# A fused recurrence and router kernel: embeddings scaled on ScalarE, tables built in the first turns, K's copy moved ahead, one idle product less

## The chip, the cores and the metric

The kernel runs on one core of one Trainium2 chip. The metric is the device time in microseconds (us), the median of several runs. Engines are named as in the profile: PE is TensorE (matmuls; PEld its weight loads), DVE is VectorE, ACT is ScalarE, POOL is GpSimd, SP is SyncE, which here issues most DMAs.

## The reference

Two blocks follow each other. The first is a linear recurrence with decay, for 4 batches, 8 heads, 768 steps and a head size of 48:

```
for t in range(S):
    cur = u * k[t] (outer) v[t]
    y[t] = r[t] @ (state + cur)
    state = w * state + k[t] (outer) v[t]
```

Its output, as 3072 tokens of 384 numbers, goes to a cosine router with 8 experts:

```
xn = x / (norm(x) + 1e-6);  en = emb / (norm(emb) + 1e-6)
logits = xn @ en.T / tau;   expert = argmax(logits)
gate = softmax(logits)[expert]
out = gate * (relu(x @ w1[expert]) @ w2[expert])
```

All is in fp32. What matters for the change is `en / tau`: the 8 rows of embeddings, each divided by its norm and by tau.

## The kernel before

The sequence is cut into 6 chunks of 128 steps; chunk and batch make 24 units. `attention` (line 842) walks over them in turns i = -1 to 23, and in each turn it writes out, by hand, the order in which the engines get their work for several units at once. Each engine works through its own instructions strictly in that order. `build_first` (line 49) comes ahead of turn -1 and starts the loads, the powers of the decay and unit 0's first products.

In turn i the pieces that matter here are, in the order of the code:

- `turn_r(i+1)`: PE turns R (L355) into a PSUM bank, DVE multiplies it by the powers (RT, L357).
- `own_rows(i, 0)` and `own_rows(i, 1)`: ACT multiplies V by the diagonal terms, four heads each (L341, four instructions). The result xd is read by `rows`.
- `turn_k(i+1)`: PE turns K (L364) into the bank "st", ACT copies it to KT (L373). That bank is also the one that `states` writes, so `states` waits for the copy.
- `scaled(i+2)` and `own(i+2)`: three POOL products of 128x384 (L312, L323, L327).
- `squares`: ACT squares rows of X (L558) for the norms, in turns 4 to 6 two a turn.
- `own_sum(i+1)`: DVE sums KU (L332).
- `sums(i)`: PE forms y (L438 with the carried state from turn 4 on, L447 with AT), ACT copies it to yT (L452).
- `states(i)`: PE (L404), into the bank "st".
- `carry(i)`: DVE adds the state (L417 or L419), POOL decays it (L420).
- `scores(i+1)`: PE (L383), 16 products. `masked(i+1, 0 and 1)`: DVE, AT (L389), twice.
- `rows(i)`: PE turns yT back (L465), DVE adds xd and writes X (L471).
- `turn_rows(i-1)`: PE turns X (L551), ACT copies it to xT (L553).

Every four turns a group of 4 units is routed: logits (L567), `choose` and `before` (DVE, L590 to L612), ranks, places, norms and lists, spread over the turns that follow. From turn 19 on the experts' weights are loaded, and after the last turn `experts` (line 1366) works through the 8 experts, almost only on PE.

Two small preparations are Python generators. Each `next` emits one step at that point of the order.

- `emb = build_experts(k)` (L233): squares and norm of the embeddings, the scaling, three PE transposes (L249) and a copy to `ent` (L250), which logits read. The steps go out in turns 1, 3 and 4.
- `tables = build_turned(k)` (L191): `no_counts` (L215, L216), `bits` (L197 to L199), `own` (L201, L202), `mask` (L205), `turned` (L206, L207) and `tie` (L210). They are all on DVE and serve the ordering of the experts in turns 19 to 21. `cum` is first read in turn 6. The steps go out in turns 4 and 5.

WAKE (line 40) is the number of idle products (L67) of 512 columns that PE does in the lead-in while the first loads are under way; each becomes two instructions.

Of the kernel before, what the change touches and what calls it, by code (L numbers as in the profile page):

```python
# [13 lines left out]
ALU = mybir.AluOpType  # L14
# [3 lines left out]
B, H, S, D = 4, 8, 768, 48  # L18
# [18 lines left out]
W_MIN, W_MAX = 0.7, 1.4  # L37
TS = 32
TG = TT // TM
WAKE = 3  # L40
AHEAD = 5
SQUARES = {1: (), 2: (), 3: (), 4: (0, 1), 5: (2, 4), 6: (3, 5)}

# [5 lines left out]
def build_first(k):  # L49
# [15 lines left out]
    def busy(columns):  # L65
        ps = k.ps.tile([128, 512], F32, name="wake", tag="y")
        nc.tensor.matmul(ps[:, 0:columns], k.ones, wide[:, 0:columns], start=True, stop=True)  # L67

    for _ in range(WAKE):
        busy(512)  # L70
# [120 lines left out]
def build_turned(k):  # L191


    nc, pool = k.nc, k.const
    no_counts(k)
    bits = pool.tile([2 * QS, 3], I32, name="bits")
    nc.vector.tensor_scalar(bits[:, 0:1], k.part, 2, E - 1, ALU.arith_shift_right, ALU.bitwise_and)  # L197
    nc.vector.tensor_scalar(bits[:, 1:2], k.part, 3, None, ALU.bitwise_and)
    nc.vector.tensor_scalar(bits[:, 2:3], k.part, 3, 4, ALU.arith_shift_right, ALU.bitwise_and)  # L199
    own = pool.tile([2 * QS, 3], F32, name="own")  # L200
    nc.vector.tensor_copy(own, bits)  # L201
    nc.vector.tensor_add(own[:, 1:2], own[:, 1:2], own[:, 2:3])  # L202
    yield
    k.mask = pool.tile([2 * QS, E], F32, name="mask")
    nc.vector.tensor_scalar(k.mask, k.number, own[:, 0:1], None, ALU.is_equal)  # L205
    nc.vector.scalar_tensor_tensor(k.turned, k.qt, own[:, 1:2], k.turned, ALU.is_equal, ALU.mult)  # L206
    nc.vector.tensor_scalar_add(k.turned, k.turned, -1.0)  # L207

    k.tie = pool.tile([128, E], F32, name="tie")
    nc.vector.tensor_scalar(k.tie, k.number, N + 1.0 / 16, None, ALU.mult)  # L210
    yield


def no_counts(k):
    k.nc.vector.memset(k.cum, 0.0)  # L215
    k.nc.vector.tensor_copy(k.cum[0:1, :], k.ebase)  # L216
# [16 lines left out]
def build_experts(k):  # L233

    nc, pool = k.nc, k.aconst
    emb, tau = k.emb_rows, k.tau_rows
    sq = k.work.tile([E, DM], F32, name="emb_sq", tag="sq")
    nrm = pool.tile([E, 1], F32, name="emb_nrm")
    nc.scalar.activation(sq, emb, ACT.Square, accum_out=nrm)
    nc.gpsimd.tensor_tensor(out=nrm, in0=nrm, in1=k.half[0:E, 0:1], op=ALU.pow)  # L240
    yield
    nc.vector.tensor_scalar_add(nrm, nrm, 1e-6)
    nc.vector.reciprocal(nrm, nrm)
    nc.vector.reciprocal(tau, tau)
    nc.vector.tensor_scalar(emb, emb, nrm, tau, ALU.mult, ALU.mult)
    yield
    ps = k.ps.tile([128, NK, E], F32, name="ps", tag="xp")
    for c in range(NK):
        nc.tensor.transpose(ps[:, c, :], emb[:, c * 128 : (c + 1) * 128], k.ident[0:E, 0:E])  # L249
    nc.vector.tensor_copy(k.ent[:, :, 0:E], ps)  # L250
    yield
# [78 lines left out]
def own_sum(k, i):  # L330
    diag = k.work.tile([128, H], F32, name="diag", tag="diag")
    k.nc.vector.reduce_sum(diag, k.KU.pop(i), axis=AX.X)  # L332
    k.diag[i] = diag


def own_rows(k, i, half):
    if half == 0:
        k.xd[i] = k.work.tile([128, H, D], F32, name="xd", tag="xd")
    diag, V = k.diag[i], k.loaded[i][2]
    for h in range(half * H // 2, (half + 1) * H // 2):  # L340
        k.nc.scalar.mul(k.xd[i][:, h, :], V[:, h, :], diag[:, h : h + 1])  # L341
# [290 lines left out]
def norms(k, g):  # L632
    k.nc.gpsimd.tensor_tensor(out=g.ssq, in0=g.ssq, in1=k.half, op=ALU.pow)
# [208 lines left out]
def attention(k):  # L842


    units = B * NCH

    def on(f, i, *more):
        if 0 <= i < units:
            f(k, i, *more)
# [5 lines left out]
    def whole(f, i, *more):  # L855
        if 0 <= i < units and i % B == B - 1:
            f(k, k.groups[i // B], *more)

    emb, tables = build_experts(k), build_turned(k)
    for i in range(-1, units):  # L860
        j = i - SETTLED * B
        if 0 < i + AHEAD < units:
            load(k, i + AHEAD)
        whole(places, i - 4)
        whole(logits_out, i - 3)
        if i >= 0:
            on(turn_r, i + 1)
        if i == 0:
            own_sum(k, i)
        if 0 < i < units - 1:  # L870
            on(own_rows, i, 0)
        if i >= 0:
            on(turn_k, i + 1)
        whole(turn_logits, i - 3)
        if i == B + 3:
            norms(k, k.groups[0])
        on(scaled, i + 2)
        if i < 0:
            own_r(k, 0)
        on(own, i + 2)  # L880
        for n in SQUARES.get(i, (i - 1,)):
            of_group(squares, n)
        if 0 < i < units - 1:
            on(own_rows, i, 1)
        if i > B + 1:
            whole(norms, i - 2)
        if j == 10:
            k.lists = turned_lists(k, perm, "tp")
            lists = taken_by_rank(k, k.lists)
            first = [Early(k, r, *lists, w) for r, w in zip(LAST, k.weights)]  # L890
        whole(choose, i - 3)
        whole(before, i - 3)
        whole(located, i - 4)
        whole(gates, i - 5)
        whole(lanes, i - 5)
        whole(listed, i - 5)
        if 0 <= i < units - 2:
            on(own_sum, i + 1)
        if i == B:
            next(emb)  # L900
        if j == 7:
            load_, count = loads(k, "xp")
        if j == 9:
            expert_of(k, by)
            number = expert_number(k, LAST[0])
            load_w1(k, number, k.weights[0][0])
        on(sums, i)
        on(states, i)
        for n in (0, 1) if i == 0 else ():
            own_rows(k, i, n)  # L910
        whole(taken, i - 6, "xp")
        whole(exps, i - 4)
        on(carry, i)
        whole(summed, i - 6)
        on(scores, i + 1)
        on(masked, i + 1, 0)
        if i == 0:
            masked(k, i + 1, 1)
        on(rows, i)
        if i != 0:  # L920
            on(masked, i + 1, 1)
        if i == units - 2:
            own_sum(k, i + 1)
            own_rows_once(k, i + 1)
        of_group(put, i)
        if j == 10:
            load_w2(k, number, k.weights[0][1])
        of_group(turn_rows, i - 1)
        whole(logits, i - 2)
        whole(ranks, i - 3)  # L930
        if i == 0:
            build_constants(k)
        if i in (1, 3):
            next(emb)
        if i in (B, B + 1):
            next(tables)
        if 3 <= i < 3 + len(k.ring):
            k.nc.gpsimd.memset(k.ring[i - 3], 0.0)
        if j == 8:
            by = order(k, load_)  # L940
        if j == 9:
            settle(k, by, count)
            perm = turner(k, by)
# [657 lines left out]
```

## Time and profile before

| | us |
|---|---|
| median of 3 runs (lowest, highest) | 408.53 (408.34, 410.69) |
| span of the profiled execution | 406.3 |
| PE busy | 388.5 |
| DVE busy | 256.2 |
| ACT busy | 172.0 |
| POOL busy | 160.5 |

A line of the timeline gives the start and the length in us, the engine, the line of the kernel, the operation, what it writes and reads with the shape, how many instructions are merged, and in brackets the idle time of the engine ahead of it and what ended it. For example the first idle products and the first scores:

```profile
1.64 4.97 PE L67 MATMUL wake<-wide,ones 128*128 128x512 f32 x6 [1.64 <-DVE wide L61]
...
8.42 1.16 PE L383 MATMUL at<-RT,KT 48*128 48x128 f32 x16 [0.18 <-DVE RT L357]
```

A line of the waits names the waiting engine, tile and line, then what ended the wait, then the total in us, how often, and the longest. Lengths of merged lines overlap at their ends, since instructions are pipelined; what a step costs its engine is the distance from its start to the next start.

### The profile page before, as it was taken

The numbers are of one execution on the slowest core, as the hardware profiler recorded it, in microseconds if no ns is written. First come the engines' busy times: TensorE is split into PE (matmuls) and PEld (weight loads), VectorE is DVE, ScalarE is ACT, GpSimd is POOL, SyncE is SP. The second block draws the span as 40 slices with busy tenths as digits, with TensorE's granted clock in tenths as the row PEclk, the third lists the DMA queues.
The fourth block names the chain that finished last, engine by engine and source line by source line (L and its number), as shares of the span: only waits on it lengthen the run. The fifth ranks groups of instructions, "written<-read, shape, count | busy, mean of one in ns | idle before, by whom it ended". The sixth has DMA issues, their size and how long they took to land.

```text
span 406.3 us, 9261 instructions
## 1 busy us (share of the span) xinstructions
PE 388.5 (96%) x3544; PEld 353.0 (87%) x3544; DVE 256.2 (63%) x604; ACT 172.0 (42%) x522; POOL 160.5 (40%) x215
## 2 busy tenths in 40 slices
PE   8979999999999999999999999999999999999980
PEld 5868888888888877899999999999999999799680
DVE  5777998878688770757667657367257266456310
ACT  3876876767677411432333232233233223232020
POOL 6996688767764332400602402401320330300220
PEclk9999999999999999999999999999999999999996
DMA  8999767767715982244706441614434340330101
GB/s 156 182 200 207 156 138 152 151 140 150 158 40 182 286 299 65 85 157 164 244 15 234 158 156 39 200 42 154 153 122 155 109 165 2 101 113 1 58 27 39
DMA packets 93800, 54.39 MB, mean 134 GB/s; under 512 B 76937, under 2 KB 88380, under 8 KB 93746
## 3 DMA queue, kind: packets, MB, share of 16 engines
q1 hardware_dynamic: 90242, 44.26, 41.0%
q0 software_dynamic: 3296, 9.44, 7.2%
q8 instruction: 30, 0.49, 0.5%
q14 instruction: 24, 0.20, 0.2%
q10 hardware_dynamic: 208, 0.00, 0.0%
HBM read 44.45 MB, written 9.63 MB: 133 GB/s over the span
## 4 chain that ended last, share of the span: by engine, by line
PE 85%; DVE 4%; SPq 3%; issue 3%; ACT 2%; DMA 1%; POOL 0%; POOLq 0%; ACTq 0%
PE ps L1217 25%; PE ps L1281 16%; PE ps L1321 5%; PE at L383 5%; PE y L447 4%; PE ps L1335 4%; PE early_h L1027 3%; PE early_y L1036 3%; PE ps L1195 3%; PE yrows L465 2%; PE y L438 2%; PE ps L1165 2%; PE rt L355 2%; PE st L404 2%; PE kt L364 2%
## 5 line engine op out<-in xcount | busy, mean ns | idle before, releaser
L1081 POOL DMA_INDIRECT out_dram<-y,to x25 | 30.0, 1199 | 173.7 <-issue 116.4
L1217 PE MATMUL ps<-xTe,w 128*128 128x192 f32 (+3 forms) x336 | 62.9, 327 | 0.0
L1217 PEld LDWEIGHTS ps<-xTe,w 128*128 128x128 f32 x336 | 55.9, 190 | 0.5
L341 ACT ACTIVATE xd<-V,diag 128x48 f32<-128x48 f32 x184 | 46.1, 324 | 0.0
L389 DVE TENSOR_TENSOR AT<-at,umask 128x512 f32<-128x512 f32 x48 | 32.7, 684 | 10.9 <-PE at L383 10.7
L1224 ACT ACTIVATE hT<-hT 128x384 f32<-128x384 f32 (+3 forms) x42 | 22.0, 523 | 32.4 <-DVE hT L1247 19.7
L1281 PE MATMUL ps<-Tw,Sh 128*128 128x192 f32 x192 | 32.5, 326 | 0.0
L1281 PEld LDWEIGHTS ps<-Tw,Sh 128*128 128x128 f32 x192 | 31.4, 190 | 0.0
L1072 POOL DMA_INDIRECT G<-xs,take x25 | 26.9, 1078 | 10.5 <-issue 4.0
L1217 PE MATMUL ps<-Tx,Sw 128*128 128x192 f32 (+3 forms) x168 | 29.7, 326 | 0.0
L383 PE MATMUL at<-RT,KT 48*128 48x128 f32 x384 | 27.9, 285 | 0.6 <-DVE RT L357 0.6
L1217 PEld LDWEIGHTS ps<-Tx,Sw 128*128 128x128 f32 x168 | 27.6, 190 | 0.1
L1234 DVE TENSOR_TENSOR u<-ps,p 128x384 f32<-128x384 f32 (+3 forms) x14 | 7.8, 558 | 31.3 <-ACT p L1231 16.6
L447 PE MATMUL y<-AT,V 128*48 128x128 f32 (+1 forms) x384 | 26.0, 278 | 0.0
L383 PEld LDWEIGHTS at<-RT,KT 48*128 48x128 f32 x384 | 23.3, 187 | 2.9 <-DVE RT L357 1.0
L327 POOL TENSOR_TENSOR KU<-KU,Rpad 128x384 f32<-128x384 f32 x24 | 24.1, 1003 | 1.8
L312 POOL TENSOR_TENSOR Kpad<-K,kpow 128x384 f32<-128x384 f32 x23 | 23.1, 1005 | 1.4 <-DVE kpow L110 1.4
L553 ACT COPY xT<-xp 128x384 f32<-128x384 f32 x24 | 11.5, 480 | 28.6 <-PE xp L551 28.6
L447 PEld LDWEIGHTS y<-AT,V 128*48 128x48 f32 (+1 forms) x384 | 19.9, 124 | 4.2 <-issue 3.6
L1281 PE MATMUL ps<-w,hT 128*128 128x192 f32 x128 | 23.4, 326 | 0.0
L323 POOL TENSOR_TENSOR KU<-K,u_bc 128x384 f32<-128x384 f32 x23 | 23.2, 1009 | 0.0
L1244 ACT ACTIVATE hT<-ps 128x384 f32<-128x384 f32 (+3 forms) x14 | 6.9, 491 | 35.7 <-PE ps L1217 35.7
(241 smaller groups left out, 820.5 us busy)
## 6 DMA issues: line engine op xcount, KB each, us to landing
w<-in_moe_w_dram SPq DMA_DIRECT2D x16, 1536.0 KB, 6.9
Rpad<-in_r_dram SPq DMA_DIRECT2D x24, 192.0 KB, 4.3
V<-in_v_dram SPq DMA_DIRECT2D x24, 192.0 KB, 4.2
xs<-X SPq DMA_DIRECT2D x24, 192.0 KB, 2.4
K<-in_k_dram SPq DMA_DIRECT2D x23, 192.0 KB, 3.8
G<-xs,take POOLq DMA_INDIRECT x27, 3.1
out_dram<-y,to POOLq DMA_INDIRECT x25, 3.9
Kpad<-in_k_dram SPq DMA_DIRECT2D x1, 192.0 KB, 3.1
```

The lines of the kernel that those rows point to most:

```text
L312: k.nc.gpsimd.tensor_mul(k.Kpad[i % len(k.Kpad)][:, :, 0:D], k.loaded[i][0], k.kpow)
L323: k.nc.gpsimd.tensor_mul(k.KU[i], k.loaded[i][0], k.u_bc)
L327: k.nc.gpsimd.tensor_mul(k.KU[i], k.KU[i], k.loaded[i][1][:, :, 0:D])
L341: k.nc.scalar.mul(k.xd[i][:, h, :], V[:, h, :], diag[:, h : h + 1])
L383: nc.tensor.matmul(at[s][:, p, :], KT[rows, p, :], RT[rows, p, :], start=True, stop=True)
L389: k.nc.vector.tensor_mul(a, k.at[i][s], k.umask[:, None, :].to_broadcast([128, NP, C]))
L447: mm(y[s][u * DP : u * DP + n, q, :], V[:, h * D : h * D + n], AT[s][:, p, :], start=(c == 0 and q == 0), stop=True, skip_group_check=True,)
L1072: nc.gpsimd.indirect_dma_start(out=G[0:n, :], out_offset=None, in_=k.xs[:, :], in_offset=IndirectOffsetOnAxis(ap=take[0:n], axis=0), bound ...
L1081: put = k.nc.gpsimd.indirect_dma_start(out=k.out[:, :], out_offset=IndirectOffsetOnAxis(ap=to, axis=0), in_=y, in_offset=None, bounds_chec ...
L1217: nc.tensor.matmul(ps[:, j, :], weights[:, (f + j) * 128 : (f + j + 1) * 128], moving, start=(first and j == 0), stop=True, skip_group_che ...
L1224: nc.scalar.activation(h, h, ACT.Relu)
L1281: nc.tensor.matmul(ps, a[:, f, :], b[:, f, :], start=(first and f == 0), stop=(f == NF // 2 - 1), skip_group_check=True)
```

## The change

Four things are moved.

- One of the three idle products of 512 columns in the lead-in is left out, so two are left.
- The scaling of the embeddings: POOL forms (norm + 1e-6) * tau, DVE takes one reciprocal in turn 2, and ACT multiplies the rows in turn 3. Two DVE instructions on single columns and one on the 8x384 rows go.
- The tables: the generator has two more stops, and its first three steps go out in turns 1, 2 and 3 between `carry` and `scores`, the last (`turned`, `tie`) at the end of turn 9. Turns 4 and 5 have none any more.
- In turns 1 to 3 K's turned copy on ACT comes ahead of both halves of `own_rows`; the second half comes after `states`.

It is meant to shorten the lead-in, to take the wait for the embeddings out of turn 4, to take DVE's load out of turns 4 and 5, and to let `states` start without a wait for the copy.

```diff
-WAKE = 3
+WAKE = 2
@@ build_turned
     nc.vector.tensor_scalar(bits[:, 2:3], k.part, 3, 4, ALU.arith_shift_right, ALU.bitwise_and)
+    yield
     own = pool.tile([2 * QS, 3], F32, name="own")
...
     nc.vector.tensor_scalar(k.mask, k.number, own[:, 0:1], None, ALU.is_equal)
+    yield
     nc.vector.scalar_tensor_tensor(k.turned, k.qt, own[:, 1:2], k.turned, ALU.is_equal, ALU.mult)
@@ build_experts
     nc.gpsimd.tensor_tensor(out=nrm, in0=nrm, in1=k.half[0:E, 0:1], op=ALU.pow)
+    nc.gpsimd.tensor_scalar(nrm, nrm, 1e-6, tau, ALU.add, ALU.mult)
     yield
-    nc.vector.tensor_scalar_add(nrm, nrm, 1e-6)
     nc.vector.reciprocal(nrm, nrm)
-    nc.vector.reciprocal(tau, tau)
-    nc.vector.tensor_scalar(emb, emb, nrm, tau, ALU.mult, ALU.mult)
+    yield
+    nc.scalar.mul(emb, emb, nrm)
     yield
@@ attention
-        if 0 < i < units - 1:
+        if B <= i < units - 1:
             on(own_rows, i, 0)
         if i >= 0:
             on(turn_k, i + 1)
+        if 0 < i < B:
+            own_rows(k, i, 0)
...
-        if 0 < i < units - 1:
+        if B <= i < units - 1:
             on(own_rows, i, 1)
...
         on(states, i)
-        for n in (0, 1) if i == 0 else ():
+        for n in (0, 1) if i == 0 else (1,) if 0 < i < B else ():
             own_rows(k, i, n)
...
         on(carry, i)
+        if i in (1, 2, 3):
+            next(tables)
...
-        if i in (1, 3):
+        if i in (1, 2, 3):
             next(emb)
-        if i in (B, B + 1):
+        if i == 2 * B + 1:
             next(tables)
```

## The prediction

> **What bounds the kernel now.** I read the windows by stage first, then the waits of TensorE (PE) in the first 60 us, then the timeline around each wait. The windows (columns: stretch, its length, then busy us and count for PE, PE weight loads, VectorE DVE, ScalarE ACT, GpSimd POOL, then clock and DMA):
>
> ```profile
> 8.40:31.00 22.60, 19.78 (x276) 17.44 (x276) 17.30 (x34) 16.30 (x61) 21.56 (x38) 1.00 1.02 193
> 31.00:48.00 17.00, 16.11 (x267) 14.16 (x267) 13.96 (x41) 11.55 (x43) 9.92 (x15) 1.00 0.84 175
> 48.00:133.00 85.00, 84.75 (x1367) 73.84 (x1365) 71.01 (x197) 61.88 (x228) 61.19 (x77) 1.00 0.63 142
> 133.00:395.00 262.00, 261.25 (x1623) 244.11 (x1622) 149.60 (x325) 78.73 (x180) 60.90 (x57) 1.00 0.38 127
> ```
>
> From 48 us to 395 us PE is idle for 1.0 us in all; then comes a tail of 11 us. So whatever PE gains or loses before 48 us should reach the end one for one, and a new stall after that is pure loss. Note POOL: 21.56 of 22.60 us in the second stretch. The waits of PE name what can be had:
>
> ```profile
> PE ps L249 <- DVE emb L245: 2.2, 1, 2.2
> PE at L383 <- DVE RT L357: 0.6, 2, 0.4
> PE st L404 <- ACT KT L373: 0.6, 1, 0.6
> PE rt L355 <- DVE X L471: 0.5, 1, 0.5
> ```
>
> Together 3.9 us, under 1% of 408.53. To these comes what the lead-in can be shortened by, since an idle product counts as busy. The largest wait has a cause that decides this case:
>
> ```profile
> 28.49 0.99 POOL L312 TENSOR_TENSOR Kpad<-K,kpow 128x384 f32<-128x384 f32 x1
> 28.58 0.13 DVE L242 TENSOR_SCALAR emb_nrm<-emb_nrm 8x1 f32<-8x1 f32 x1
> ...
> 29.24 1.40 DVE L245 TENSOR_SCALAR emb<-emb,emb_nrm,tau 8x384 f32<-8x384 f32 x1 [0.29 <-DVE tau L244]
> 29.44 0.99 POOL L323 TENSOR_TENSOR KU<-K,u_bc 128x384 f32<-128x384 f32 x1
> ...
> 30.51 1.00 POOL L327 TENSOR_TENSOR KU<-KU,Rpad 128x384 f32<-128x384 f32 x1
> ```
>
> L245 (8x384) ran 1.40 us and ended at 30.64, just in the gap between POOL's L323 (ends 30.43) and L327 (30.51). It passed the border between L312 and L323 at 29.48 without getting in. L242, one element wide, ran freely beside L312. The tables' steps do the same in turns 4 and 5:
>
> ```profile
> 35.44 1.00 POOL L323 TENSOR_TENSOR KU<-K,u_bc 128x384 f32<-128x384 f32 x1
> 36.10 0.36 DVE L216 COPY cum<-ebase 1x8 f32<-1x8 f32 x1
> 36.52 1.01 POOL L327 TENSOR_TENSOR KU<-KU,Rpad 128x384 f32<-128x384 f32 x1
> 36.67 0.88 DVE L201 CAST own<-bits 128x3 f32<-128x3 int32 x1
> ```
>
> **What the Trainium skill says.** "SBUF — State Buffer", section "SBUF: two separate sides": VectorE and GpSimd share a port pair under an exclusive lock, held for the whole instruction; a VectorE op in a 2-port mode, or with two SBUF inputs while GpSimd reads SBUF, is blocked. The trace agrees: both ops above end within 0.2 us of a POOL end. "VectorE: DVE Perf Modes", section "What auto-detection actually checks": the 2-port mode needs one SBUF source and an even (or equal) outer dimension; the 0.13 us of L242 agrees. "ScalarE: Activation LUTs", section "What ACT_TABLE_LOAD costs": 186 ns + 0.833 ns per element, and 93 ns per pointer operand. "TensorE: Matmul & The Clock Gate", section "What's actually happening": half clock until an activity window of about 3.4 us was busy, the window running free of the program. The trace agrees: the 512-wide idle products start 0.85 us apart (2.65, 3.50, 4.36, 5.21), while later 192-wide ones take 0.16 us each, about twice the rate per column.
>
> **The change part by part.** I write gains (+) in PE time.
>
> *One idle product less.* It removes two instructions of 0.85 us, 1.7 us of PE. K's turn could start at 5.2 instead of 6.44 (first K landed 3.1 us after 1.36, at 4.5). At half clock its four products take 0.85 us, so DVE's KT goes to 6.3 (kp is done at 5.91), RT to 6.9, the first scores from 8.42 to 7.6. But the next PE step, rt of unit 1 (9.52), needs R1. K1 (issued 3.64) landed 4.5 us later, at 8.16, and R2 at 12.28; R1, V1, K2 and R2 share that gap, so R1 lands at about 9.2 to 9.3. Gain +0.2, not 0.8. POOL's first Kpad (8.91) goes to 8.2, where K1 lands: POOL moves 0.7 us ahead of PE's 0.2. Bounds: 0 to +0.9 (a late clock change, from which the shorter lead-in gains more).
>
> *K's copy first in turns 1 to 3.* ACT does L373 before four L341 (0.9 us). In turn 2 states (L404) started at 20.54; after sums at 18.90 and 0.97 us for them it could be 19.87: +0.67. In turn 3, 25.11 against 23.96 + 0.97: +0.18. Together +0.85. The moved half rows now stand behind yT; they end 0.3 us before X (L471) needs them by my count (21.6 against 21.9 in turn 2), so they cost nothing.
>
> *Embeddings' scaling on ACT.* L242, L244, L245 leave DVE; one L243 (0.15, one element, free) stays. POOL gets one 8x1 op: between 0.12 (a small memset) and 0.26 (L84); 0.15 taken. ACT gets one 8x384 product: 0.52 from its neighbour L239, or 0.60 by the skill's price; 0.5 taken. It stands behind xT of turn 3, so ps (L249) waits at most 0.15 us. The 2.2 us go. But turn 4's ACT queue is then full: from the start of xp it is 0.53 to xT, then 0.38 xT, 0.47 scaling, 0.91 rows, 0.47 KT, 1.02 two squares, 0.90 rows, 0.62 yT, so yrows (L465) starts at 5.34; PE by itself is there after 4.67. Before, xp to yrows took 34.18 - 27.23 = 6.95. Gain 1.6, not 2.2.
>
> *Tables out of turns 4 and 5.* The first RT wait (0.38, turn 5) goes, but the same ACT sum without scaling is 4.87, exactly what turn 5 takes now (34.62 to 39.49), and yrows there already starts 0.04 us after yT. Gain 0. The X wait of turn 6 (0.52) goes: without 1.8 us of tables DVE reaches its AT before the scores end. Gain +0.5.
>
> *Tables into turns 1 to 3.* Each step stands after carry, in an idle time of 0.5 to 0.7 us that DVE has there waiting for scores (17.27, 22.33, 26.89). By length they fit (0.2 to 0.3 us unblocked). But L216, L201 and L205 are of the kind that POOL blocks, and POOL never idles there: one gap of 0.08 us a turn, between L323 and L327. Who misses it waits up to 2 us. Behind the blocked step stand AT, X, AT and RT; PE's sums need the second AT, and it can come 0.4 us late for free (24.09 against 24.5). With POOL 0.7 and PE 0.2 ahead: L216 comes at about 16.36; POOL's last gap between memsets is at 16.3, the next gap at 18.4. Missed: AT 1.5 late, PE -1.25. Caught: then L201 comes at 20.6, gap at 22.6, AT 1.35 late, PE -0.9. If the first is missed, PE's delay brings the second to its gap for nothing. So about -1.1 either way. L205 in turn 3 comes at 26.0 to 26.2, the gap at 26.1: 0 taken, -1.2 if missed.
>
> *The last tables' step in turn 9.* L206, L207, L210 come after AT (ends 63.43), where DVE idles 0.48 until RT, while POOL runs L312, L323, L327 from 62.96 to 66.02:
>
> ```profile
> 63.91 0.69 DVE L357 TENSOR_TENSOR RT<-rt,rpow 128x512 f32<-128x512 f32 x1 [0.48 <-PE rt L355]
> 63.92 1.02 POOL L323 TENSOR_TENSOR KU<-K,u_bc 128x384 f32<-128x384 f32 x1
> 65.02 1.00 POOL L327 TENSOR_TENSOR KU<-KU,Rpad 128x384 f32<-128x384 f32 x1
> 65.41 0.69 DVE L598 TENSOR_TENSOR seq<-oh,first 128x32 f32<-128x32 f32 x1
> 68.81 0.66 PE L355 MATMUL rt<-ident,Rpad 128*128 128x128 f32 x4
> ```
>
> L598, with two SBUF inputs, ran 0.69 us and ended with L327 at 66.1: blocked too, so L206 will be. It gets in before L327, L207 after it: RT starts at 66.1 instead of 63.91 (65.5 if POOL is 0.6 earlier there, as a shorter DVE queue in turns 6 to 8 makes it). Behind it stand choose and before (1.7 us), diag, carry, AT, X; X ended at 68.75 and rt waits for it at 68.81, so there is no slack. PE loses 0.9 (1.5 at worst, 0 if nothing blocks): 0.9 taken.
>
> **Sum.** The timed 408.53 is 2.2 us more than the profile's span; I take that as constant. +0.2 + 0.85 + 1.6 + 0 + 0.5 = 3.15; less 1.1 and 0.9: net 1.15 us. 408.53 - 1.15 = 407.4.
>
> **The rivals.**
> Rival 1, *the tables cost nothing*: each step finds a gap. For it: DVE idles at each place and the timings miss by under 0.1 us. Against it: in the trace, blocked is the rule. 408.53 - 3.15 = 405.4; with the largest lead-in gain 404.7.
> Rival 2, *the port waits pile up*, slower: the first step missed (1.25), the third too (1.2), the last at its worst (1.5), the second free. 3.95 - 3.15 = 0.8 slower: 409.3. For it: POOL's 95% in turns 1 to 3. Against it: three misses in a row.
> Rival 3, *the clock comes late*: with 3.57 us of idle products instead of 5.3 a window is no longer surely filled, and PE stays at half clock for one more window. It costs at most half of 3.4 us, less about 0.5 that PE waits anyway: 1.2 on top of the forecast, 408.6. Against it: the turns follow closely and load the array.
>
> **How the numbers follow.** Forecast (406.6 to 408.2) 0.52, rival 1 (under 406.6) 0.22, rival 2 (over 408.2) 0.18, rival 3 0.08. The range 405.2 to 409.4 takes in the middle of rival 1 and the centres of 2 and 3. Faster by over 1% means under 404.4: all gains whole, no loss, 0.04. Slower by over 1% needs over 412.6, more than rival 2 and 3 together (410.5): 0.03. Within 1%: 0.93.
>
> **What would show it.** Right: the waits of PE lose ps<-emb and st<-KT; yrows<-yT appears in turn 4 (about 0.6 us); L216 or L201 lasts over 1 us in turns 1 or 2 with a sums or y wait on AT; L207 lasts near 1 us at about 62 us and a wait on X follows. Wrong: all table steps under 0.3 us (rival 1), rt of unit 1 before 9.2, or transposes 0.2 us apart after 7 us (rival 3).

## The result, and the profile after

| | before | after |
|---|---|---|
| median of 6 runs, us (lowest, highest) | 408.45 (408.25, 410.69) | 405.80 (405.16, 406.02) |
| ratio, 95% interval | | 0.9917 [0.989, 0.9944] |
| span of the profiled execution, us | 406.3 | 403.8 |

The change saved 2.65 us where 1.15 were forecast. The time lies inside the stated range, at its lower end, and 1.6 below the 407.4 of the forecast. In the changed kernel the code of the turns stands two lines lower (the transposes of R are L357 for L355, the first AT product L449 for L447); the scaling of the embeddings is L247. In the experiments below the line numbers shift by a few with each edit.

First the same four stretches as before, cut at the same instructions of PE (columns as before: stretch, length, busy us and count of PE, weight loads, DVE, ACT, POOL, then clock and DMA):

```profile
7.57:27.87 20.30, 19.33 (x276) 17.56 (x276) 17.27 (x38) 14.61 (x52) 18.89 (x35) 1.00 1.12 202
27.87:44.40 16.53, 16.32 (x267) 14.17 (x267) 11.78 (x31) 13.52 (x52) 13.60 (x19) 1.00 0.99 205
44.40:130.10 85.70, 84.71 (x1363) 73.81 (x1361) 71.35 (x200) 62.10 (x230) 60.53 (x76) 1.00 0.62 141
130.10:392.10 262.00, 261.27 (x1623) 244.13 (x1622) 149.53 (x325) 78.76 (x180) 61.12 (x57) 1.00 0.38 127
```

The first stretch starts 0.83 us earlier (7.57 for 8.40), is 2.30 shorter (20.30 for 22.60), the second 0.47 shorter, the third 0.70 longer, the last is the same. That adds up to 2.90. The third stretch is the only loss. PE's last product ends 2.88 us earlier (391.73 for 394.61); the span is only 2.5 shorter, since what follows that product took 12.1 us for 11.7. The waits of PE that are left:

```profile
PE rt L357 <- DMA Rpad<-in_r_dram: 0.7, 1, 0.7
PE ps L251 <- ACT emb L247: 0.2, 1, 0.2
PE at L385 <- DVE RT L359: 0.2, 1, 0.2
...
PE rt L357 <- DVE X L473: 0.8, 1, 0.8
```

The 2.2 for the embeddings, the 0.6 of `st` for KT and the 0.5 for X in turn 6 have gone. Two are new: 0.7 at the transposes of R for unit 1, which have to wait for R to land, and 0.8 at those before turn 11. The next lines are the timeline where the forecast expected the table steps to be blocked, one group for each of turns 1, 2 and 3:

```profile
16.32 0.12 POOL L187 MEMSET fresh<- 128x40 f32 x1
...
16.47 0.16 DVE L218 COPY cum<-ebase 1x8 f32<-1x8 f32 x1
...
16.50 0.11 POOL L188 MEMSET fresh<- 128x8 f32 x1
...
20.04 0.58 POOL L242 TENSOR_TENSOR emb_nrm<-emb_nrm,half 8x1 f32<-8x1 f32 x1
...
20.63 0.16 DVE L202 CAST own<-bits 128x3 f32<-128x3 int32 x1
20.74 0.26 POOL L243 TENSOR_SCALAR emb_nrm<-emb_nrm,tau 8x1 f32<-8x1 f32 x1
...
24.93 1.64 DVE L206 TENSOR_SCALAR mask<-number,own 128x8 f32<-128x8 f32 x1
...
25.52 1.03 POOL L325 TENSOR_TENSOR KU<-K,u_bc 128x384 f32<-128x384 f32 x1
...
26.48 0.68 DVE L391 TENSOR_TENSOR AT<-at,umask 128x512 f32<-128x512 f32 x1
```

In turn 1 the copy L218 took 0.16 us: it fell into the gap between two memsets. In turn 2 the cast L202 took 0.16 as well, in the gap between POOL's power and the small product L243 that follows it, an instruction which the change itself had brought in. POOL's next large product starts only at 21.07; in the kernel before it follows the power at once. Only the mask of turn 3 was blocked, 1.64 us, until POOL's L325 ended at 26.55. It made AT late, and PE did not feel it: ahead of the first product with AT, turn 4 has the embeddings' transposes and 16 products with the carried state (L440). Two more traces of the changed kernel, on other chips, show the same (copy 0.16 and 0.21, cast 0.16 and 0.16, mask 1.59 and 1.64). In turn 9 the forecast and the trace agree:

```profile
59.62 1.01 POOL L325 TENSOR_TENSOR KU<-K,u_bc 128x384 f32<-128x384 f32 x1
...
59.74 0.97 DVE L208 SCALAR_TENSOR_TENSOR turned<-qt,own,turned 128x64 f32<-128x64 f32 x1
...
60.75 1.02 DVE L209 TENSOR_SCALAR turned<-turned 128x64 f32<-128x64 f32 x1
...
61.77 0.68 DVE L359 TENSOR_TENSOR RT<-rt,rpow 128x512 f32<-128x512 f32 x1
...
65.94 0.66 PE L357 MATMUL rt<-ident,Rpad 128*128 128x128 f32 x4 [0.76 <-DVE X L473]
```

Each of the two steps ends with a product of POOL. RT starts 2.15 us after the transposes of R, where the kernel before has 0.69, so it is about 1.5 us late. The wait of 0.76 comes out at the transposes of R for the next turn but one.

### The profile page after: what moved, and what is told of

It is laid out like the page before. It is cut to its first block, busy times and chain, and to the rows that moved or that the text cites. A ratio compares the mean times of both kernels' runs of the same rounds, so it can differ in the third digit from the quotient of the medians.

```text
span 403.8 us, 9257 instructions
## 1 busy us (share of the span) xinstructions
PE 387.4 (96%) x3542; PEld 352.9 (87%) x3542; DVE 254.3 (63%) x601; ACT 172.6 (43%) x523; POOL 161.1 (40%) x216
## 4 chain that ended last, share of the span: by engine, by line
PE 83%; ACT 3%; issue 3%; POOL 3%; DVE 2%; DMA 2%; SPq 1%; POOLq 0%; ACTq 0%
PE ps L1223 25%; PE ps L1287 16%; PE ps L1327 5%; PE at L385 4%; PE y L449 4%; PE ps L1341 4%; PE early_h L1033 3%; PE early_y L1042 3%; PE ps L1201 3%; PE yrows L467 3%; PE ps L1171 2%; PE y L440 2%; PE rt L357 2%; PE kt L366 2%; PE xp L553 2%
## 5 line engine op out<-in xcount | busy, mean ns | idle before, releaser
L449 PE MATMUL y<-AT,V 128*48 128x128 f32 (+1 forms) x384 | 26.0, 277 | 0.0
L449 PEld LDWEIGHTS y<-AT,V 128*48 128x48 f32 (+1 forms) x384 | 19.9, 124 | 4.1 <-issue 3.8
L325 POOL TENSOR_TENSOR KU<-K,u_bc 128x384 f32<-128x384 f32 x23 | 23.3, 1012 | 0.0
```

The source lines that it names most:

```text
L325: k.nc.gpsimd.tensor_mul(k.KU[i], k.loaded[i][0], k.u_bc)
L449: mm(y[s][u * DP : u * DP + n, q, :], V[:, h * D : h * D + n], AT[s][:, p, :], start=(c == 0 and q == 0), stop=True, skip_group_check=True,)
```

## Experiments: each part alone

Four kernels take one part of the change each. Of the kernel before, 62 runs were made on this chip, with a median of 409.48 us. Here the first loads land about 1 us later than on the first chip, so the lead-in is longer in all kernels.

**Idle product alone.**

```diff
-WAKE = 3
+WAKE = 2
```

> The kernel before with one idle product less and nothing else. Theory (PE is held by fixed events of others: R of unit 1 landing at about 9.4 us, and GpSimd's gap before which the embeddings' scaling L245 can't run): PE's rt of unit 1 starts within 0.1 us of 9.52, so the lead-in itself gives under 0.1; but GpSimd starts its chain 0.6 us earlier (8.3 instead of 8.9), is never idle until turn 4, and so its gap comes 0.6 earlier: L245 ends at about 30.0 instead of 30.65, and PE's wait for it falls from 2.2 to about 1.6. Net gain 0.6 us. Rival A (the lead-in's 0.8 us at the first scores carries through): gain 0.8 already at 9.5 us. Rival B (nothing, all is DMA): gain under 0.1 at the end.

409.5 us, ratio 0.9997 [0.9978, 1.0016]. The first scores come at 7.36, but the transposes of R for unit 1 then wait 1.9 us, to 10.44. The lead-in ends with a landing, not with PE. This trace puts the wait down to POOL's first scaled K, but in 19 of the 20 traces of this case, this one among them, the transposes start 0.14 us after R has landed (in the kernel before 0.22), while POOL's product ends anywhere from 0.19 before them to 0.44 after. The 0.6 us that my theory expected from an earlier gap of POOL did not come: the wait for the embeddings is still 1.8 here.

**K's copy first alone.**

```diff
-        if 0 < i < units - 1:
+        if B <= i < units - 1:
             on(own_rows, i, 0)
...
+        if 0 < i < B:
+            own_rows(k, i, 0)
...
-        for n in (0, 1) if i == 0 else ():
+        for n in (0, 1) if i == 0 else (1,) if 0 < i < B else ():
             own_rows(k, i, n)
```

> The kernel before with K's copy first in turns 1 to 3 and nothing else. Theory: PE is 0.9 us ahead after turn 3, but the scaling L245 in turn 4 still ends in GpSimd's gap at about 30.6, so PE's wait for it grows from 2.2 to about 3.1 and the net is 0 (within 0.2). Rival (gains of parts add up): 0.9 faster, the wait stays at 2.2.

410.45 us, ratio 1.0025 [1.0001, 1.0048]: nothing gained. Its waits for KT are gone, and its wait for the embeddings has grown from 2.2 to 3.1. The timeline of this kernel says why:

```profile
29.08 2.34 DVE L245 TENSOR_SCALAR emb<-emb,emb_nrm,tau 8x384 f32<-8x384 f32 x1 [0.30 <-DVE tau L244]
29.26 1.00 POOL L312 TENSOR_TENSOR Kpad<-K,kpow 128x384 f32<-128x384 f32 x1
...
30.22 1.00 POOL L323 TENSOR_TENSOR KU<-K,u_bc 128x384 f32<-128x384 f32 x1
...
31.29 1.00 POOL L327 TENSOR_TENSOR KU<-KU,Rpad 128x384 f32<-128x384 f32 x1
...
31.57 0.24 PE L249 MATMUL ps<-ident,emb 8*128 8x8 f32 x1 [3.13 <-DVE emb L245]
```

The scaling on DVE was issued early and lasted 2.34 us. In the kernel before it took 1.40. Its end is set by the gap ahead of POOL's L327, so whatever PE gains before turn 4 is handed back there.

**Embeddings' scaling on ScalarE alone.**

```diff
+    nc.gpsimd.tensor_scalar(nrm, nrm, 1e-6, tau, ALU.add, ALU.mult)
...
-    nc.vector.tensor_scalar_add(nrm, nrm, 1e-6)
...
-    nc.vector.reciprocal(tau, tau)
-    nc.vector.tensor_scalar(emb, emb, nrm, tau, ALU.mult, ALU.mult)
+    yield
+    nc.scalar.mul(emb, emb, nrm)
...
-        if i in (1, 3):
+        if i in (1, 2, 3):
             next(emb)
```

> The kernel before with the embeddings' scaling on ScalarE and nothing else. Theory: the 2.2 us wait goes and up to 0.3 of a new wait on ScalarE (emb or yT) takes its place: 1.9 us faster, give or take 0.3 for where the tables of turns 4 and 5 now fall against GpSimd's gaps. Rival (the prediction's ACT sum, yrows waiting for both halves of yT): a wait of yrows for yT of 0.6 us in turn 4 and 1.6 us faster.

407.42 us, ratio 0.9941 [0.9916, 0.9965]. The wait for the embeddings is 0.20; those of 0.55 for KT and 0.52 for X stand as before. The rival's wait of 0.6 for yT is not there.

**Table steps alone.**

The generator has its two more stops here too (two added `yield`s).

```diff
         on(carry, i)
+        if i in (1, 2, 3):
+            next(tables)
...
-        if i in (B, B + 1):
+        if i == 2 * B + 1:
             next(tables)
```

> The kernel before with the tables in turns 1, 2, 3 and 9 and nothing else. Theory: with the old timing the cast of turn 2 comes at about 21.6, inside GpSimd's L312, and lasts 1.5 us; PE loses about 0.45 there, but the wait for the embeddings in turn 4, fixed by GpSimd's gap, shrinks by as much. Turns 5 and 6 give about 0.7, the step of turn 9 takes about 0.75 back (a wait of rt on X at about 69 us). Net 0, within 0.3. Rival (the steps are hidden wherever DVE has idle time): no long cast, no wait in turn 11, 0.7 to 0.9 faster.

409.28 us, ratio 0.9995 [0.9975, 1.0015]. Here the cast of turn 2 lasted 1.41 us and PE waited 0.24 for AT. The waits of turns 5 and 6 are gone, one of 0.76 before turn 11 has come, and the wait for the embeddings (1.8) lies between and evens out what came earlier.

The medians move by +0.0, +1.0, -2.1 and -0.2 us, together -1.3. The whole change gives more than its parts. That is not the work of the clock, which takes a share in these medians (see below): among the runs with a mean clock of 0.988 or more (the share of full speed that TensorE was granted over a run; it is about 0.99 without any disturbance, since the idle end counts at half clock) the parts move by -0.1, -0.1, -1.6 and +0.1, together -1.7, and the whole change, on another chip, by -2.4.

## Experiments: where the forecast was wrong

**The changed kernel again**, on the chip of three of the experiments that follow (before there: 410.44 us).

> The changed kernel again, as the measure for the others on this chip. Both theories: 2.6 to 3.2 us faster than before, mean granted clock at 0.989 or more in every run, while of the runs of before about 45% have 0.988 or less (each extra window of half clock costs 1.5 us).

407.21 us, ratio 0.992 [0.9893, 0.9947].

**The gap between memsets taken away.** Eight memsets (`caps`) go from turn 0 to turn 12, so that POOL begins its products some 0.2 us earlier relative to DVE.

```diff
-    for i, cap in enumerate(CAPS):
-        nc.gpsimd.memset(k.caps[:, i : i + 1], float(cap))
...
+        if i == 3 * B:
+            for n, cap in enumerate(CAPS):
+                k.nc.gpsimd.memset(k.caps[:, n : n + 1], float(cap))
```

> The changed kernel with GpSimd's eight small memsets of caps (0.27 us) moved from turn 0 to turn 12, nothing else. Theory (a table step costs by whether it meets a gap of GpSimd): GpSimd is 0.27 us earlier in turn 1, the gap between its last two memsets passes before the copy L218 arrives, L218 waits for the end of two GpSimd products and lasts 1.5 to 2.0 us instead of 0.16; PE waits about 1.2 us for AT in turn 2; 1.0 to 1.2 us slower than the changed kernel. Rival (the steps are cheap because DVE idles there; GpSimd's phase is of no matter): same time within 0.2, L218 short.

407.24 us, that of the changed kernel. The copy missed the gap and lasted 0.84 us, but it got in at the border of two products after one of them (POOL's L312 ran from 17.07 to 18.07, the copy from 17.25 to 18.09). PE did not wait, though the steps of turns 2 and 3 were blocked in this trace too, for 1.00 and 1.30 us. My theory, that a missed step waits for a pair of products, fell.

**The gap missed by more.** The same with the memsets of `sums` and `fresh` moved as well, so that the copy comes 0.42 us after the start of a product and not 0.18 (another chip, before there: 410.01 us).

```diff
-    nc.gpsimd.memset(k.sums, 0.0)
-    nc.gpsimd.memset(k.fresh, 1.0)
-    nc.gpsimd.memset(k.fresh[:, :, 0:1], 0.0)
...
+        if i == B + 1:
+            k.nc.gpsimd.memset(k.sums, 0.0)
+            k.nc.gpsimd.memset(k.fresh, 1.0)
+            k.nc.gpsimd.memset(k.fresh[:, :, 0:1], 0.0)
```

> The changed kernel with the memsets of caps, sums and the ones taken out of turn 0 and put at the ends of turns 5 and 12, so that GpSimd begins the first product of turn 1 some 0.6 us earlier and VectorE's one-element copy of the tables is issued about 0.5 us after the start of that product. Theory (a VectorE operation that needs the shared access gets in at the end of the running product when it was issued in the product's first 0.2 us, and one product later when it was issued after 0.35 us or more): the copy lasts 1.3 to 1.6 us, across the border of the two products; AT of turn 2 is masked 0.7 to 1.0 later; TensorE waits 0.1 to 0.6 us at the second half of y in turn 2, and the time is 0 to 0.5 above the changed kernel. Rival A (the copy gets in at the next border in any case): it lasts 0.5 us and nothing moves. Rival B (what the prediction counted, a wait for a pair of products and no slack): 1.1 us slower than the changed kernel.

```profile
17.05 1.00 POOL L309 TENSOR_TENSOR Kpad<-K,kpow 128x384 f32<-128x384 f32 x1
...
17.47 1.56 DVE L213 COPY cum<-ebase 1x8 f32<-1x8 f32 x1
...
18.00 1.01 POOL L320 TENSOR_TENSOR KU<-K,u_bc 128x384 f32<-128x384 f32 x1
...
19.09 1.00 POOL L324 TENSOR_TENSOR KU<-KU,Rpad 128x384 f32<-128x384 f32 x1
...
20.92 0.32 PE L444 MATMUL y<-AT,V 128*64 128x128 f32 x2 [0.41 <-DVE AT L386]
```

Now the copy took 1.56 us, past the border at 18.0 and into the gap at 19.01 to 19.09. AT was masked 0.9 later and PE waited 0.41; by its starts it lost 0.6 in this turn. Time 407.44 us, ratio 0.9931 [0.9912, 0.9949]. That is a miss as the forecast imagined it, and it costs PE 0.6 and not 1.25: of the 1.4 us by which the copy is late, DVE had some 0.4 idle, and PE needs the second half of AT later still.

**Load order.** V of the first unit goes behind K and R of the second.

```diff
+    if i == 1:
+        nc.sync.dma_start(out=k.loaded[0][2], in_=k.v[0, :, 0:C, :].rearrange("h s d -> s h d"))
+    if i != 0:
+        nc.sync.dma_start(out=V, in_=of(k.v))
-    nc.sync.dma_start(out=V, in_=of(k.v))
```

> The changed kernel with the load of unit 0's V put behind K and R of unit 1, so that R of unit 1 lands one load (0.95 us) earlier. Theory (the lead-in's gain is lost in the wait of rt for that load): the wait of 0.74 us goes, PE is 0.7 us ahead from rt of unit 1 on and keeps it: 0.7 us faster than the changed kernel. Rival (another limit stands close behind: GpSimd's scaled K, or V of unit 0, which now lands later): under 0.2 faster.

406.36 us, ratio 0.9897 [0.9869, 0.9925], 0.85 under the changed kernel. The transposes of R for unit 1 start at 9.46 for 10.57, and PE is 0.90 ahead at 67 us and 0.63 at its end.

**PE kept busy in its wait.** The kernel before, with eight idle products of 128 columns in the wait for the embeddings.

```diff
+    idle = k.ps.tile([128, 512], F32, name="wake", tag="xp")
+    for _ in range(8):
+        nc.tensor.matmul(idle[:, 0:128], k.ones, k.ones, start=True, stop=True)
```

> The kernel before with eight idle products of 128 columns (1.7 us of PE) put into PE's wait for the embeddings in turn 4. They shorten nothing. Theory (the wait of 2.2 us is what drops PE's clock to half for one or more windows of 3.4 us in 45% of the runs of before): no run, or nearly none, with a mean clock of 0.988 or less; the fastest runs as before (within 0.2), the mean over runs 0.8 us lower. Rival (the clock drops for another reason): the same share of low-clock runs as before.

409.54 us against 410.44 (ratio 0.9967 [0.9951, 0.9983]). No wait got shorter, and the fastest runs are alike (409.17, 409.28). Of 23 runs of the kernel before, 14 had a mean clock of 0.987 or less; of the 20 runs of this one, none. A long wait of PE can thus cost more than its length: in some executions the clock falls behind it. The trace of K's copy first alone caught it (last columns: clock, DMA share, GB/s):

```profile
28.00:32.00 4.00, 0.86 (x11) 0.63 (x9) 3.67 (x7) 3.37 (x14) 3.92 (x6) 0.91 1.22 248
32.00:36.00 4.00, 4.00 (x51) 3.55 (x52) 0.75 (x4) 0.75 (x2) 0.29 (x1) 0.50 1.01 214
36.00:42.00 6.00, 6.00 (x51) 5.27 (x51) 3.76 (x13) 2.29 (x7) 3.78 (x5) 0.54 0.50 105
```

After its wait of 3.1 us PE ran at half clock from 31.3 to 41.6 us. This is why that kernel is not the same as before but 1 us slower by its median: 16 of its 20 runs have a mean clock of 0.987 or less, against 24 of 62 of before on that chip, and the other runs of the two have medians of 409.01 and 409.06.

## Experiments: one part undone, and better versions

The changed kernel on one more chip (before: 409.94 us) and three kernels beside it:

> The changed kernel itself, beside the kernels that undo one part of it each. Both theories: 2.4 to 3.4 under the kernel before, ratio 0.992, waits of TensorE of 0.2 for the embeddings and 0.75 for the rows of turn 10.

406.75 us, ratio 0.9915 [0.989, 0.994].

**Embeddings back on VectorE**, all else changed (the diff of their part above, reversed):

> The changed kernel with the embeddings' scaling back on VectorE, all else as changed. Theory (the release of the embeddings is set by the gap between GpSimd's products and not by TensorE, so whatever the other parts gain before turn 4 becomes wait): the wait for the embeddings is 2.6 to 3.2, the time within 0.7 of the kernel before on either side, and most runs have low-clock windows. Rival (the parts add, and this one is worth 1.6 to 2.1): 0.6 to 1.1 under the kernel before, wait 2.2 or less.

410.25 us, ratio 0.9998 [0.9976, 1.0019]: without this part the other three are worth nothing. Among the runs with a mean clock of 0.988 or more it is so too (409.01 for both kernels); the other 14 of its 20 runs have one of 0.987 or less. The profiled wait for the embeddings was 1.8, less than I expected, because the clock had already fallen once after the wait for R and PE was 1.6 us late. The windows show both stretches at a lower clock:

```profile
12.00:16.00 4.00, 4.00 (x49) 3.79 (x46) 1.49 (x4) 2.85 (x11) 3.84 (x5) 0.59 1.25 197
...
32.00:36.00 4.00, 4.00 (x53) 3.53 (x55) 1.01 (x4) 1.83 (x8) 0.66 (x1) 0.57 1.16 232
```

**The idle product back.**

```diff
-WAKE = 2
+WAKE = 3
```

> The changed kernel with three idle products in the lead-in, not two. Theory (the lead-in ends with the landing of R of the second unit, so an idle product more fits into the wait for it): the time of the changed kernel within 0.2, the wait at the transposes of R for turn 1 shorter by 0.6 to 0.9, TensorE from there on at the same times. Rival (the idle product is worth its length): 0.5 to 0.9 above the changed kernel.

406.75 us, the same. The wait for R is 1.2 for 1.8, and PE goes on from there at the same times within 0.2. This part of the change does nothing.

**K's copy back behind the rows** (another chip, before: 410.01):

```diff
-        if B <= i < units - 1:
+        if 0 < i < units - 1:
             on(own_rows, i, 0)
...
-        if 0 < i < B:
-            own_rows(k, i, 0)
...
-        for n in (0, 1) if i == 0 else (1,) if 0 < i < B else ():
+        for n in (0, 1) if i == 0 else ():
             own_rows(k, i, n)
```

> The changed kernel with one part undone: K's turned copy goes back behind the row-wise product of R in turns 1 to 3, everything else stays. Theory (K's copy first is worth 0.95 in turns 1 to 3, and did nothing by itself on the kernel before because the wait for the embeddings behind it grew by as much; with the scaling on ScalarE that wait is 0.2): the wait of st for K's copy is back at 0.5 to 0.6 in turn 2, that for the embeddings is 0, and the time is 0.6 to 0.9 above the changed kernel. Rival (the order of the copies is worth nothing, as by itself): the time of the changed kernel within 0.2.

408.13 us, ratio 0.9959 [0.9944, 0.9974]. The wait of 0.55 for KT is back, and in turn 3 PE waits 0.29 at y, put down by the trace to the embeddings' reciprocal on DVE; against the changed kernel PE is 1.2 late by turn 3. The wait for the embeddings stayed at 0.20. I had expected 0.6 to 0.9 in time; by its ratio against 0.9915 it is about 1.8, by PE's starts 1.2. Not all of that is K's copy. With PE later, the cast of turn 2 comes beside a large product of POOL: the cast took 0.71 us (22.50) and the step behind it 0.91 (23.24), 0.16 to 0.18 each in the changed kernel on other chips. The second half of AT is late by that, and PE's sums of turn 3 take 1.4 us for 0.9.

**Table steps back** in turns 4 and 5:

> The changed kernel with the table steps put back at the ends of turns 4 and 5. Theory (from the two traces: the steps in turns 1 to 3 cost nothing, out of turns 4 and 5 they give 0.6, the last one in turn 9 costs 0.75): TensorE's wait of 0.75 before turn 11 is gone, waits of about 0.5 before turn 7 and 0.2 at the first scores of turn 5 are there instead; the time is 0.15 under the changed kernel, 0 to 0.3. Rival (the prediction's figures: steps in turns 1 to 3 cost 1.1): 1.0 to 1.5 under it. Second rival (the table move is a gain inside the changed kernel): 0.3 or more above it.

407.59 us, 0.84 above the changed kernel beside it. My theory said 0.15 below. Among the runs with a mean clock of 0.988 or more the difference is 0.89 (407.49 and 406.60). The trace of this one execution agreed with the theory, apart from a stretch of half clock after the wait for R: without those 1.56 us PE would have been 0.26 ahead after turn 11, once the 0.21 by which it left the lead-in earlier is taken off too. So I repeated the pair with the load order that makes that wait short (before on that chip: 409.91):

> The changed kernel with V of the first unit loaded behind K and R of the second, beside the same with the table steps put back. Both theories: 0.8 under the changed kernel, ratio 0.9885 to 0.991; wait for R of the second unit 0.3 to 0.9.

406.11 us, ratio 0.9901 [0.9871, 0.9931]. Its trace shows one thing more, in turn 2:

```profile
20.48 0.58 POOL L242 TENSOR_TENSOR emb_nrm<-emb_nrm,half 8x1 f32<-8x1 f32 x1
...
20.81 0.16 DVE L202 CAST own<-bits 128x3 f32<-128x3 int32 x1
```

Here the cast lies inside POOL's power of one column, not in a gap, and was not held. So in turn 2 it is enough that no large product of POOL is running. The same kernel with the table steps back:

> The same load order, with the table steps back at the ends of turns 4 and 5. Theory (the 0.8 lay in TensorE's clock after the long wait in the lead-in, and the steps are worth what the waits say: 0.6 gained in turns 5 and 6, 0.75 lost in turn 11): the time of w1_order within 0.4, rather below it. Rival (the table move is worth 0.8 for a reason that the waits don't show): 0.5 to 1.0 above w1_order, with no half clock before TensorE's end.

406.67 us, 0.56 above it, ratio 0.9921 [0.99, 0.9943]. No run of either kernel has a mean clock under 0.988, and every run of this one lies above every run of the other. So it was not the clock. The trace has a reason in turn 4:

```profile
32.77 0.99 POOL L315 TENSOR_TENSOR Kpad<-K,kpow 128x384 f32<-128x384 f32 x1
...
33.37 1.38 DVE L216 COPY cum<-ebase 1x8 f32<-1x8 f32 x1
...
34.81 1.00 POOL L330 TENSOR_TENSOR KU<-KU,Rpad 128x384 f32<-128x384 f32 x1
...
35.94 0.68 DVE L360 TENSOR_TENSOR RT<-rt,rpow 128x512 f32<-128x512 f32 x1
...
36.68 0.38 PE L386 MATMUL at<-RT,KT 48*128 48x128 f32 x2 [1.39 <-DVE RT L360]
```

The copy (eight elements of one partition) missed a border again (0.60 us after the start of L315), lasted 1.38 us, the cast behind it 0.87, and PE waited 1.39. At its end PE is 1.05 late; this trace is of a run of 406.98 and the other of one of 405.70, so the 0.56 of the medians is the figure to go by. In the trace of the kernel with the table steps back and the old load order the same copy met the gap and took 0.16. What the table steps cost hangs on where GpSimd is when they come, in turns 4 and 5 as in turns 1 to 3; the time of that kernel fits a miss in most executions, but no trace of such a one shows it.

**The two waits that are left, taken away** (the chip of K's copy back). The subtraction L209 is folded into the compare that reads the table, and `tie` goes ahead of `turned`:

```diff
-    nc.vector.scalar_tensor_tensor(k.turned, k.qt, own[:, 1:2], k.turned, ALU.is_equal, ALU.mult)
-    nc.vector.tensor_scalar_add(k.turned, k.turned, -1.0)
...
     nc.vector.tensor_scalar(k.tie, k.number, N + 1.0 / 16, None, ALU.mult)
+    nc.vector.scalar_tensor_tensor(k.turned, k.qt, own[:, 1:2], k.turned, ALU.is_equal, ALU.mult)
...
-    nc.vector.tensor_scalar(perm, k.turned, rank, None, ALU.is_equal)
+    nc.vector.tensor_scalar(perm, k.turned, -1.0, rank, ALU.add, ALU.is_equal)
```

> The changed kernel with the last table step of turn 9 shortened: the subtraction of 1 from the turned table (1.03 us on VectorE beside GpSimd's products) is folded into the one compare that reads the table later. Theory (TensorE's wait of 0.75 for the rows of turn 10, seen in every profile of the changed kernel at the transposes of R for turn 11, is VectorE's lateness by exactly these two steps): the step takes 0.98 us instead of 1.99, the wait shrinks from 0.75 to under 0.1, and the time falls by 0.65 to 0.75 against the changed kernel (some 3.3 to 3.5 under the kernel before, where the changed kernel is 2.6 to 2.9 under it). Rival (the wait has another cause, or the time is taken back later, as it was by the wait for the embeddings): the wait stays or a later one grows by as much, and the time is that of the changed kernel within 0.2.

406.15 us, ratio 0.992 [0.9886, 0.9953]. The wait of 0.75 before turn 11 is gone; PE's start there is 0.95 earlier than in the changed kernel's last trace, on another chip, 0.2 of it from the lead-in. The ratio, with its wide interval, can't tell 0.7 us. With the load order as well:

> The changed kernel with both improvements that its profile points to: the subtraction folded into the compare, and V of the first unit loaded behind K and R of the second. Theory (the two waits, for the first rows of R and for the rows of turn 10, lie one after the other on TensorE and nothing between takes their gain back; the load order alone gave 0.85): 1.4 to 1.7 under the changed kernel, ratio to the kernel before 0.986 to 0.989. Rival (the gain of the load order, which is only 0.63 at TensorE's end, and that of the fold overlap): 0.8 to 1.0 under the changed kernel.

405.06 us against 410.01, ratio 0.9875 [0.9822, 0.9929], as my theory had it, and faster than the kernel before. The changed kernel did not run on this chip; its ratios elsewhere, 0.9915 to 0.992, lie inside the interval, so the times alone don't separate the two. The traces do: PE's last product ends at 391.1 us, in the three traces of the changed kernel at 391.7, 392.9 and 393.1. The waits of its PE, in the whole span:

```profile
PE wake L67 <- DVE wide L61: 1.6, 1, 1.6
PE xp L554 <- ACT xT L556: 0.2, 1, 0.2
PE rt L358 <- DMA Rpad<-in_r_dram: 0.2, 1, 0.2
PE ps L249 <- ACT emb L245: 0.2, 1, 0.2
```

## Why the prediction was right and wrong

Right in kind: PE's starts set the time, nothing after 70 us changes, and the waits that went and came are nearly those named. By the starts of PE in the two traces of the first chip, each term of the sum was (gains positive, us):

| step of the prediction | said | measured | from |
|---|---|---|---|
| one idle product less | +0.2 | +0.02 | rt of unit 1 at 9.50 for 9.52 |
| K's copy first | +0.85 | +1.1 | `st` of turn 3 at 23.98 for 25.11 |
| scaling on ACT | +1.6 | +1.8 | lead of 3.16 at `ps`, 2.92 after yrows |
| tables out of turn 5 | 0 | +0.2 | lead of 3.11 after yrows of turn 5 |
| tables out of turn 6 | +0.5 | +0.5 | lead of 3.60 at rt of turn 6 |
| tables into turns 1 to 3 | -1.1 | 0 | no wait for AT in turns 1 to 4 |
| last step in turn 9 | -0.9 | -0.7 | lead of 2.87 at 65.94 |
| sum | +1.15 | +2.9 | end of PE 2.88 earlier |

- **The step that failed** is "Tables into turns 1 to 3 ... So about -1.1 either way": it measured 0. The mechanism, steps of DVE that wait for POOL, was right: one of three was blocked for 1.64 us, and in turn 9 the two steps took 2 us. Its size was wrong, in two terms. The first is "POOL never idles there: one gap of 0.08 us a turn". With the first step caught, the cast was to come at 20.6 and to wait for a gap at 22.6. It came at 20.63 and took 0.16 us, as POOL had only work on one column from 20.04 to 20.99: the power, which stood in turn 2 before the change too, and the small product that the change adds, which I had counted only as 0.15 us of POOL's time (it took 0.26, and makes a gap). The second is the price of a miss: a wait of "up to 2 us" with 0.4 us of slack behind it, hence -1.25 and -0.9. The mask of turn 3 missed its gap and was held 1.64 us at no cost to PE, where the forecast has -1.2 for a miss; so was the copy of the first memset experiment for 0.84, and the copy that took 1.56 us cost PE 0.6.
- **Rival 1** was the nearer case, and its 405.4 is 0.4 from the measured time, but in part by luck: it has nothing for the step of turn 9, which cost 0.7, and the gains that it sums to 3.15 came to 3.6.
- **K's copy first** gave 1.1 for 0.85. The 0.97 us that I took for `sums` was from a turn that seems to hold a small wait for KT itself: in the changed kernel it is 0.92 (18.76 to 19.68), and turn 1 gained 0.08, where I counted none.
- **The scaling on ACT** was put 0.2 too low: I let yrows wait for both halves of yT (0.62), but in turn 4 its first transposes start with the first half. The trace has yT written from 30.78 to 31.39 and yrows started at 31.18, and PE's lead falls only from 3.16 to 2.92 over the four of them. ACT's product itself took 0.61 us, in agreement with the 0.60 that I had estimated from the prices in "ScalarE: Activation LUTs" of the Trainium skill, section "What ACT_TABLE_LOAD costs"; my 0.5 from the neighbour was too low, and the wait at `ps` is 0.20 for 0.15. The same mistake probably hid the 0.2 of turn 5; that was not tried by itself.
- **The idle product** came out in the direction stated and even smaller: PE waits for R to land, and putting the product back costs nothing.
- **Not in the forecast at all**: the clock. On the chip where the embeddings were put back, the medians differ by 3.2 us, but the runs with a mean clock of 0.988 or more by 2.4 (409.0 and 406.6). About 0.8 of the gain there is half clock that the kernel before suffers after its 2.2 us wait. On the first chip, where four of six runs of before lie at 408.25 to 408.53, hardly any of it is in the 2.65. Rival 3 looked for a late clock in the lead-in of the changed kernel; a stretch of half clock there is seen in two experiments, after waits for R of 1.87 and 2.03 us, and in no profile of the changed kernel itself, though 3 of its 13 runs on the chip where the embeddings were put back have a mean clock of 0.984 and take about 1.9 us more than the others. In the compared pair on the first chip the full clock came at 5.95 us before and at 6.02 after, so Rival 3 did not happen there.
- **That single parts don't add**, I didn't forecast either. The wait for the embeddings was released by POOL and not by PE, so it returned every gain made ahead of it. My order of summing, with that wait taken out once for all, was right for the whole change only.

## What to carry over

A wait that is released by an engine outside the chain gives back whatever is gained ahead of it: take that wait away first, and judge the other parts with it gone. Where two engines compete for one access, don't price a moved instruction with the worst wait; look up which gap it falls into, count the gaps that the change itself makes, and take the slack of the reader behind it. An instruction that may be blocked is best made shorter or folded away, as moving it only changes which gap it has to meet.

## What the runs showed of the hardware

- "SBUF — State Buffer" of the Trainium skill, section "SBUF: two separate sides", says that whichever of the two starts first keeps the port pair for its whole instruction. These traces add what happens at the border between the first two of POOL's three large products. Some steps got in at the end of the first: a copy issued 0.18 us after its start (0.84 us long) and casts issued 0.32 and 0.79 us after it (0.71 and 0.23). Others did not, and ended in the next gap of 0.08 us, ahead of a product that reads the result of the one before it: copies issued at 0.42 and 0.60 us (1.56 and 1.38), a cast at 0.57 (1.41), and the mask of turn 3 at 0.33 to 0.41 in eight traces (1.59 to 1.66). The time since the start of the product doesn't sort the cases, and the cause of the difference is open.
- The cast was not held by POOL's power of one column: in three traces with the changed load order it lies inside the 0.58 us of the power and took 0.16. That is as exact as POOL's spans in the profile, but it is not what the rule of that section would lead one to expect.
- "TensorE: Matmul & The Clock Gate" of the Trainium skill, section "What's actually happening", puts the return to half clock after at least one idle window of about 3.4 us. Here it took less: waits of PE of 1.8 to 2.2 us were enough in part of the executions: 14 of 23 runs of the kernel before had a mean clock of 0.987 or less, and with idle products in the wait none of 20. The length agrees: a stretch at half clock lasted 3.41 us in the clock's record of three traces, once three times as long (10.24), and one of 3.41 made PE about 1.6 us late.
- The landing of the first loads differed by about 1 us between chips (R of unit 1 at 9.37 on the first, 10.44 on another), so a lead-in that ends with a landing is judged best by the starts of PE after it.
